# A spectral filter beside a gated feed-forward layer: half-length inverse products over the columns, a separate path for column 256, and 64x64 tiles for the 32-point steps

## Chip, cores and metric

One core of one Trainium2 chip. The metric is device microseconds (us) of one execution; each kernel is run several times, and each run has a state, fast or slow. Engines: PE is TensorE, DVE is VectorE, ACT is ScalarE, POOL is GpSimd, SP is SyncE, which here only issues DMAs.

## The reference

```python
def reference(A_x, A_w_r, A_w_i, B_x, B_w_gate, B_w_up, B_w_down):
    # x: (1, 2048, 512) bf16; w_r, w_i: (2048, 257); gate, up: 512 x 1792; down: 1792 x 512
    xn = layernorm(A_x)
    X = rfft2(xn)                                   # over tokens (2048) and columns (512)
    a = irfft2(X * (w_r + 1j * w_i), s=(2048, 512))
    g, u = xn @ B_w_gate, xn @ B_w_up
    return A_x + a + (gelu(g) * u) @ B_w_down       # tanh gelu
    # [types, casts and the set-up of the inputs are cut]
```

## The kernel before

The feed-forward part is a regular stream on PE: for each of four blocks of 512 tokens and each of 14 slices of the inner width a gate group, then an up group (four matmuls of 512 columns each), with the down groups in between. The Fourier part is cut into units, placed at numbered gaps of this stream, called **hooks** (0 to 156). In a trace, hook n is where the stream's n-th group ends.

- D: forward transform over the 512 columns (real input: 257 frequencies, kd).
- A: 64-point step over the tokens. Its result goes to a scratch in HBM and is read back transposed (`tv`).
- B: 32-point step, ends the forward transform. Then the filter on DVE. C: 32-point step, starts the inverse; second trip through HBM (`vv`).
- E: 64-point step; F: inverse transform over kd; DVE adds the result.

```python
def load_late(dst, src, keys):                      # later loads: GpSimd's queue, not before the PE work ahead of it
    op("pool", lambda e: e.dma_start(dst, src), w=keys, dma=True, after=[("pe", pr.cnt["pe"])])

def unit_A(j):
    ...                                             # [matmuls cut]
    op("act", ... activation(t4[:], pair(bk), ACT.Copy, scale=SC_A), ...)
    dma("sp", scr1.rearrange(...)[j], t4[:], r=[("tt", j % 4)], w=[("scr1", j)])
    if j >= 3:
        load_tv(j - 3)                              # [the last three after j = 15]

def unit_B(h):                                      # 128x64 tiles, two at once
    for ri in range(2):
        for hh in range(2):
            e.matmul(bank(bk + ri)[64 * hh:64 * hh + 64, 0:257], be[:, 64 * ri:64 * ri + 64], tv[:, 16 * hh + h, :], ...)
    # waits for all of tv; then ACT evicts, and DVE makes two products and two sums with Wr, Wi

def unit_C(h):                                      # 64x128 tiles, two at once
    for ri in range(2):
        for hh in range(2):
            e.matmul(bank(bk + hh)[:, 0:257], cm[64 * hh:64 * hh + 64, h, ri, :], y[64 * hh:64 * hh + 64, ri, 0:KD], ...)

def unit_F(j):                                      # four products of 256 columns
    e.matmul(bank(bk)[:, 0:256], z[:, 0, :], gm[:, 0, :], ...)
    e.matmul(bank(bk)[:, 0:256], z[:, 1, :], gm[:, 1, :], ...)
    e.matmul(bank(bk)[:, 256:512], z[:, 2, :], gm[:, 2, :], ...)
    e.matmul(bank(bk)[:, 256:512], z[:, 3, :], gm[:, 3, :], ...)

# places: filter loads (16 of them, on GpSimd) from hook 26; the first B at 54, C from 61, E from 113, F from 117
xv = A_x.rearrange("o (q b j) d -> b q (o j) d", b=2, j=NJ)   # order of tokens: runs of j are contiguous in HBM
```

## Time and profile before

| | before |
|---|---|
| time, median of the runs taken with the changed kernel's | 196.56 us (196.11 to 200.26, 4 runs, the longest of them slow) |
| span of the profiled run, granted clock | 194.3 us, 1.0 |
| PE busy | 186.9 us, 96% |
| last hook (156) ends at | 188.2 us |
| filter loads | 16, issued by GpSimd |

Read it in this order: busy share per engine (who could be the bound), the 40 slices (where it isn't), the waits (who stops whom), then the timeline of the bound engine for the real price of its instructions. The prediction shows those lines.

### The profile page before, as it was taken

How to read it: one execution, taken by the hardware profiler on the slowest of the kernel's cores; microseconds unless marked ns; L12 is line 12 of the kernel's file. 1: busy time of each engine (PE TensorE's matmuls, PEld its weight loads, DVE VectorE, ACT ScalarE, POOL GpSimd, SP SyncE). 2: the span in 40 equal slices, each digit the busy share in tenths (PEclk: the TensorE clock that was granted, in tenths of full speed). 3: DMA queues.
4: the chain of work that ended last, by engine and by line, in shares of the span. 5: the costliest groups of instructions: out<-in, count | busy, mean ns of one | idle time of the engine just before them, and what ended most of it. 6: DMA issues, size and time to landing. Idle time of an engine off the chain costs nothing.

```text
span 194.3 us, 3181 instructions
## 1 busy us (share of the span) xinstructions
PE 186.9 (96%) x1173; PEld 95.4 (49%) x1173; DVE 112.1 (58%) x266; ACT 89.1 (46%) x160; POOL 26.3 (14%) x52
## 2 busy tenths in 40 slices
PE   7599898999999999999999999999999999999993
PEld 2285454646454444444444444444455555555562
DVE  2759899787722227658577556423146656546361
ACT  3144465666466124547446363413454555644310
POOL 0200515023200232222300000000011011111000
DMA  4999999556655663355862331340002221121112
GB/s 125 326 290 333 285 255 255 144 145 129 139 162 142 145 119 90 75 95 129 177 168 86 108 112 35 104 120 17 1 0 54 54 59 27 42 53 45 26 28 54
DMA packets 19167, 23.09 MB, mean 119 GB/s; under 512 B 2240, under 2 KB 16832, under 8 KB 18768
## 3 DMA queue, kind: packets, MB, share of 16 engines
q1 hardware_dynamic: 16064, 16.46, 31.4%
q0 software_dynamic: 1712, 5.32, 12.5%
q10 hardware_dynamic: 1376, 1.11, 2.0%
q8 instruction: 9, 0.15, 0.3%
q14 instruction: 6, 0.05, 0.1%
HBM read 16.57 MB, written 6.31 MB: 118 GB/s over the span
## 4 chain that ended last, share of the span: by engine, by line
PE 85%; DVE 7%; DMA 4%; issue 1%; SPq 1%; POOL 1%; ACT 0%; DVEq 0%
PE ps L642 24%; PE ps L600 22%; PE ps L585 22%; DMA wu<-in_B_w_up_dram 4%; DVE st L351 3%; PE ps L462 2%; PE ps L488 2%; PE ps L522 2%; PE ps L622 2%; DVE hT L606 1%; PE ps L373 1%; SPq L304 1%; PE ps L437 1%; PE ps L548 1%; PE ps L550 1%
## 5 line engine op out<-in xcount | busy, mean ns | idle before, releaser
L606 DVE TENSOR_TENSOR hT<-ps,gl 128x512 bf16<-128x512 f32 (+1 forms) x59 | 39.0, 662 | 38.5 <-PE ps L600 36.9
L585 PE MATMUL ps<-xnT,wg 128*128 128x512 f16 (+1 forms) x236 | 58.1, 369 | 0.8 <-ACT xnT L385 0.8
L600 PE MATMUL ps<-xnT,wu 128*128 128x512 f16 (+1 forms) x236 | 58.1, 368 | 0.2 <-DMA wu<-in_B_w_up_dram 0.2
L588 ACT ACTIVATE gl<-ps 128x512 bf16<-128x512 f32 (+1 forms) x59 | 34.0, 575 | 45.0 <-PE ps L585 44.0
L642 PE MATMUL ps<-wd,hT 128*128 128x512 bf16 x210 | 50.1, 379 | 0.0
L600 PEld LDWEIGHTS ps<-xnT,wu 128*128 128x128 bf16 x236 | 22.4, 98 | 21.9 <-issue 0.8
L585 PEld LDWEIGHTS ps<-xnT,wg 128*128 128x128 bf16 x236 | 21.8, 98 | 21.8 <-issue 2.8
L642 PEld LDWEIGHTS ps<-wd,hT 128*128 128x128 bf16 x210 | 19.8, 98 | 21.1 <-issue 0.8
L657 DVE TENSOR_TENSOR x_sb<-ps,x_sb 128x512 bf16<-128x512 f32 x12 | 8.3, 690 | 16.4 <-PE ps L642 16.4
L530 POOL COPY zt<-xn 1x128 bf16<-1x128 bf16 x16 | 4.9, 309 | 80.4 <-DMA xn<-row 42.5
L556 ACT ACTIVATE eo<-ps 128x512 bf16<-128x512 f32 x16 | 9.5, 595 | 12.4 <-PE ps L551 12.4
L529 ACT ACTIVATE zt<-ps 128x512 bf16<-128x512 f32 x16 | 9.5, 596 | 7.7 <-PE ps L522 7.6
L468 ACT ACTIVATE xc<-ps 128x514 f16<-128x514 f32 x16 | 8.7, 600 | 8.8 <-PE ps L462 8.8
L351 DVE BATCH_NORM_STATS2 st<-x_sb 128x6 f32<-128x512 bf16 x16 | 10.8, 684 | 3.0 <-DMA x_sb<-in_A_x_dram 3.0
L494 ACT ACTIVATE vp<-ps 128x514 bf16<-128x514 f32 x16 | 8.7, 598 | 6.2 <-PE ps L488 6.2
L561 DVE TENSOR_TENSOR ys<-eo 128x256 bf16<-128x256 bf16 x16 | 4.6, 289 | 11.9 <-ACT eo L556 11.9
L447 ACT ACTIVATE tt<-ps 128x514 f16<-128x514 f32 x16 | 8.7, 597 | 6.0 <-PE ps L441 6.0
L420 ACT ACTIVATE xs<-ps 128x512 f16<-128x512 f32 x16 | 9.6, 597 | 4.1 <-PE ps L416 4.1
L359 POOL TENSOR_TENSOR rstd<-vpe,mhalf 128x4 f32<-128x4 f32 (+1 forms) x5 | 4.6, 921 | 31.0 <-DVE vpe L358 31.0
L308 POOL DMA_DIRECT2D Wr<-in_A_w_r_dram x8 | 5.0, 625 | 19.2 <-PE ps L642 13.4
L363 DVE TENSOR_SCALAR xn<-x_sb,ag,rstd 128x512 f16<-128x512 bf16 x16 | 6.2, 435 | 2.0 <-POOL rstd L359 2.0
L308 POOL DMA_DIRECT2D Wi<-in_A_w_i_dram x8 | 4.9, 617 | 13.0 <-PE ps L585 10.1
(68 smaller groups left out, 169.6 us busy)
## 6 DMA issues: line engine op xcount, KB each, us to landing
scr<-tt SPq DMA_DIRECT2D x16, 128.5 KB
tv<-scr SPq DMA_DIRECT2D x16, 128.5 KB
scr<-vp SPq DMA_DIRECT2D x16, 128.5 KB
arena<-scr SPq DMA_DIRECT2D x16, 128.5 KB
out_dram<-osb SPq DMA_DIRECT2D x30, 64.0 KB
x_sb<-in_A_x_dram SPq DMA_DIRECT2D x6, 256.0 KB, 14.1
Wr<-in_A_w_r_dram POOLq DMA_DIRECT2D x8, 128.5 KB, 4.7
Wi<-in_A_w_i_dram POOLq DMA_DIRECT2D x8, 128.5 KB, 4.3
```

The costliest lines, as they stand in the source:

```text
L308: op("pool", lambda e: e.dma_start(dst, src), w=keys, dma=True, after=[("pe", pr.cnt["pe"])])
L351: op("dve", lambda e: e.bn_stats(st[:, j, :], x_sb[:, j, :]), r=[("x", j, 0), ("x", j, 1)], w=[("st", j)])
L420: op("act", lambda e: e.activation(x4[:].rearrange("p (a c r) -> p a c r", a=2, r=4), bank(bk).rearrange("p (a r c) -> p a c r", a=2, r=4) ...
L447: op("act", lambda e: e.activation(t4[:], pair(bk), ACT.Copy, scale=SC_A), r=[("ps", bk), ("ps", bk + 1)], w=[("tt", j % 4)])
L468: op("act", lambda e: e.activation(xc[s2][:, :, 0:KD], pair(bk), ACT.Copy, scale=SC_B), r=[("ps", bk), ("ps", bk + 1)], w=[("xc", s2)])
L529: op("act", lambda e: e.activation(z[:], bank(bk).rearrange("p (a c) -> p a c", a=4), ACT.Copy, scale=SC_E), r=[("ps", bk)], w=[zk])
L556: op("act", lambda e: e.activation(o2[:], bank(bk), ACT.Copy), r=[("ps", bk)], w=[ok])
L585: ins = e.matmul(bank(bg)[:, 0:n], wg_sb[:, dc, fc * P:(fc + 1) * P], xnT[:, dc, c0:c0 + n], start=(dc == 0), stop=(dc == 3))
L588: op("act", lambda e: e.activation(gl[k % 3][:, 0:n], bank(bg)[:, 0:n], ACT.Gelu_apprx_tanh), r=[("ps", bg)], w=[("gl", k % 3)])
L600: ins = e.matmul(bank(bu)[:, 0:n], wu_sb[:, dc, fc * P:(fc + 1) * P], xnT[:, dc, c0:c0 + n], start=(dc == 0), stop=(dc == 3))
L606: op("dve", lambda e: e.tensor_tensor(hT[b % 2][:, fc, h0:h0 + n], bank(bu)[:, 0:n], gl[k % 3][:, 0:n], ALU.mult), r=[("ps", bu), ("gl", k ...
L642: ins = e.matmul(bank(bk), hT[b % 2][:, fc, jj * P:(jj + 1) * P], wd_sb[:, fc, :], start=(fc == 0), stop=(fc == NFC - 1))
```

## The change

The intent is to give PE less to stream. F folds a second time: with all angles taken half a sample off, the 256 outputs of each parity follow from 128 columns and their mirror, so its products have 128 columns. Column 256 would spoil the even sizes, so it is taken out of the main path and walks a narrow one of its own ("mini", four small steps). With 256 columns left, B and C fit 64x64 tiles, four at a time; B of a slice and C of the slice before share a hook, so PE changes its tiling less often. The filter is loaded in eight slices, once for the rows of the real parts and once for those of the imaginary parts; the loads now go out on SP's queue. The four loads of C's constants (256 KB each, on GpSimd) move too, from hooks 34, 52, 62 and 72 to hooks 46 to 52. To make the halves of a tile neighbours, the order of tokens changes.

```diff
-    xv = A_x.rearrange("o (q b j) d -> b q (o j) d", b=2, j=NJ)
+    xv = A_x.rearrange("o (q j b) d -> b q (o j) d", b=2, j=NJ)
 [constants, buffers and the narrow path cut]
+        def load_tv(m):                                   # once per four units of A
+            for r in range(2):
+                dma("sp", tv[64 * r + 16 * m:64 * r + 16 * m + 16]..., scr1[8 * m:8 * m + 8, 64 * r:64 * r + 64]..., ...)
+        def load_W(s):                                    # 8 loads a slice, 64 in all
+            for k, src in enumerate((A_w_r, A_w_i)):
+                for c in range(2):
+                    for i in range(2):                    # the same rows of HBM twice
+                        p0 = 64 * c + 32 * i
+                        yield (load_late, W[k][s % 4][p0:p0 + 32, :, :, 0:KW], v[c][:, :, hs, :], ..., "sp")
 unit_B
+                        ins = e.matmul(bank(bk + r)[64 * c:64 * c + 64, 256 * hh:256 * hh + 256], be[64 * r:64 * r + 64, 0:64],
+                                       tv[64 * r:64 * r + 64, 16 * c + 2 * g + hh, :], ...)
 unit_F
+                for a in range(4):
+                    ins = e.matmul(bank(bk)[:, a * P:(a + 1) * P], z[:, a, :], gm[:, a, :], ...)
 places
+        for s, h0 in enumerate((26, 31, 36, 41, 55, 60, 66, 71)):     # filter slices
+        for g in range(9):
+            h = int(52 + 5.5 * g)                         # B of slice g and C of slice g - 1
-            at(113 + 2.5 * j, (unit_E, j))
+            at(107 + 2.5 * j, (unit_E, j))
```

## The prediction

> **What bounds the kernel now.** I read the page first: busy time per engine, the 40 slices, the chain that ended last.
>
> ```profile
> PE 186.9 (96%) x1173; PEld 95.4 (49%) x1173; DVE 112.1 (58%) x266; ACT 89.1 (46%) x160; POOL 26.3 (14%) x52
> ...
> PE   7599898999999999999999999999999999999993
> ...
> DVE  2759899787722227658577556423146656546361
> ...
> PE 85%; DVE 7%; DMA 4%; issue 1%; SPq 1%; POOL 1%; ACT 0%; DVEq 0%
> ```
>
> TensorE (PE) is busy in every slice after the first 30 us or so; VectorE (DVE) is near full only in slices 3 to 8 (10 to 40 us), where layer norm and fold run. The waits agree: what idle time there is belongs to ACT and DVE, waiting for PE; the rows in which PE waits sum to about 4 us (1.7+1.2+0.8+0.5+0.2), and in stretches of ten us PE is busy 10.00 from 40 us to 190. So time is saved here only by giving PE less to stream, and only after about 40 us surely.
>
> PE's busy time overlaps itself (matmuls are pipelined), so a matmul's own duration is not its price. The price is the distance from one start to the next, and that is read from the timeline of PE. A stretch with the inverse transform (L522 is the E step, L548 to L551 the F step over kd):
>
> ```profile
> 151.46 0.39 PE L522 MATMUL ps<-be,arena 128*128 128x128 f16 x4
> 151.69 1.03 PE L585 MATMUL ps<-xnT,wg 128*128 128x512 f16 x4
> 152.55 1.03 PE L600 MATMUL ps<-xnT,wu 128*128 128x512 f16 x4
> 153.41 0.27 PE L548 MATMUL ps<-gm,zt 128*128 128x256 f16 x1
> 153.52 0.27 PE L549 MATMUL ps<-gm,zt 128*128 128x256 f16 x1
> 153.63 0.27 PE L550 MATMUL ps<-gm,zt 128*128 128x256 f16 x1
> 153.74 0.27 PE L551 MATMUL ps<-gm,zt 128*128 128x256 f16 x1
> 153.85 1.03 PE L585 MATMUL ps<-xnT,wg 128*128 128x512 f16 x4
> ```
>
> Columns: start, length, engine, line. 512 columns cost (152.55-151.69)/4 = 0.216 us, 256 columns 0.11 us, 128 columns (151.69-151.46)/4 = 0.057 us. A stretch with the 32-point steps (L462 is B in 128x64 tiles, L488 is C in 64x128 tiles):
>
> ```profile
> 83.80 0.81 PE L585 MATMUL ps<-xnT,wg 128*128 128x512 f16 x3
> 84.53 0.63 PE L462 MATMUL ps<-tv,be 128*64 128x257 f16 x8
> 85.10 1.04 PE L600 MATMUL ps<-xnT,wu 128*128 128x512 f16 x4
> ...
> 86.84 1.03 PE L600 MATMUL ps<-xnT,wu 128*128 128x512 f16 x4
> 87.80 0.62 PE L488 MATMUL ps<-yy,cm 64*128 64x257 bf16 x8
> 88.35 1.04 PE L585 MATMUL ps<-xnT,wg 128*128 128x512 f16 x4
> ```
>
> Eight matmuls of 257 columns take 0.57 us, not 8 x 0.11: two tiles run at once, so there are four waves of 0.11. And each visit to a tile shape has a toll: B should start at 83.80+3x0.216 = 84.45 and starts at 84.53 (0.08), and stays 0.57-0.44 = 0.13 longer than its waves: 0.21 us. For C 0.10+0.11, the same 0.21.
>
> **What the Trainium skill says.** "TensorEngine Tiling (Array Packing)", section Tiling Modes: a 64x64 split gives four independent tiles, and changing the tiling mode (not just the tile) drains the engine. The trace agrees on the drain: 0.21 us per visit. It shows two tiles at once, never four. "TensorE: Matmul & The Clock Gate", section Part 3, says tiles of different row and column groups overlap and reports 3.07x for four row tiles; no run here shows it for 64x64. The same tiling page, section Tile-to-Partition Mapping, says column tiling turns off the fast weight load; in the trace before, the 128x64 weight loads last 109 ns against 98 ns for 128x128 and delay nothing. "VectorE: DVE Perf Modes", section Mode 2x_1P, asks for 16-bit data, step +1 or -1 and 4-byte alignment for two results a cycle; the adds here (256 columns 0.29 us, 512 0.425, 1024 0.685) run at 0.52 ns an element, which fits two a cycle. The new mirrored write has step -1 and may or may not keep it.
>
> **The change part by part, on PE.**
> 1. F: 64 matmuls go from 256 to 128 columns. Same count, all late, all in a saturated stretch: 64 x (0.11-0.057) = **-3.4 us**.
> 2. B: 64 matmuls remain, but four at once instead of two: 32 waves become 16. 16 x 0.11 = **-1.8 us**, if four tiles really run at once.
> 3. C: 64 matmuls in pairs become 128 of half the width in fours: 32 waves before and after, 0.
> 4. Visits. Before: A in 8 pairs, B 8, C 8, the row of column 256 once: 25. After: A in 4 groups; B of a slice and C of the slice before it stand in one hook and share the 64x64 shape: 9 visits, the second of the four narrow steps among them; the three other narrow steps: 3. 16. 9 x 0.21 = **-1.9 us**. A's four (0.8 us) fall before 63 us, partly where PE waits for DVE anyway; I count half: -1.5.
> 5. The narrow path of column 256: 4+4+16+1 matmuls of 16 to 64 columns, in 2+1+4+1 waves, one row matmul removed: seven waves. I take the 128-column price, 0.057 us, as the price of one: **+0.4 us**.
> Sum: -3.4-1.8-1.5+0.4 = -6.3 us. D, E, the gate, up and down matmuls (47+48+46 us of stream by the starts) are unchanged.
>
> **Beside PE.** DVE: the filter was 16 x (2x0.425+2x0.29) = 22.9 us and becomes 16 products of 1024 elements, 16 x 0.69 = 11 us, the combining sum having moved into C's products. The finish gets two more half-width operations per tile, 32 x 0.29 = 9.3 us (11.5 if the mirrored one runs at one element a cycle), plus about 2 us of narrow work. Even, within 2 us. It moves work from 80-115 us to 135-180 us, where DVE was at 5.2 to 5.7 us in ten; about four tiles in ten us add 2.3 to 2.8: at most 8.5 in ten. Not the bound. ACT: 48 evictions of 0.60 us become 24 of 1024 elements; from 0.597 for 512 and 0.383 for 256 the slope is 0.84 ns an element, so 1.02 us each: 24.5 us instead of 28.7. Fewer, but each holds two PSUM banks longer, and B and C now queue two of them at one hook.
>
> **Rivals.**
> (a) *Four tiles don't run at once*, or their weight loads (twice as many per column streamed) don't keep up. If both steps went at the present pair rate, B saves nothing and C's 64 waves cost 3.5 us more: gain about 1 us, time near 195. For it: nothing here shows four at once. Against it: A, B and C all reach full pair overlap with loads issued 2 to 4 ns apart. One in seven.
> (b) *A DMA round trip becomes the wait.* B needs all of the transposed tile, E all of the second one, and both now come sooner after their last producer. E: C's last unit moves from about 123 to about 121.5 us on the old clock, and E's first from 137 to 132. From C's end: eviction to 123.5, write issued 124 and landed about 3 us later (the old last read went out at 129.6 after a write issued at 125.6), read issued and landed about 3.2 us after: 130.3. Slack 1.7 us. B: last A at 62.5, second eviction 64.1, write landed 67, two reads behind the filter's loads, landed 70.8; B's hook is at 71.6. Slack 0.8 us. The 64 filter loads now go out by SP's queue, at 0.36 to 0.6 us of issue each (30 us in all) in the same stretch, in order, ahead of those reads. A stall of 1 to 3 us is possible: one in five.
> (c) *PSUM banks.* With B and C in one hook ACT owes 2 us; the next gate's gelu is 2 us late. Four banks remain, which last PE two gates and two ups, 3.4 us. No stall, or a few tenths.
> (d) *The early stretch moves.* x is now read in rows of 1 KB instead of 2 to 4 KB; packets of 1024 bytes took about 50 ns and 4096 about 200, so bytes count and not packets. I expect +-0.3 us.
>
> **Range.** The sum says -6.3; I put -0.4 us of it back for small stalls of (b), (c) and (d): 196.4-5.9 = 190.5 us, 3% faster. The good end is all tolls saved and nothing lost: 188.9. The bad end is one stall of (b) or half of (a): 193.6. The 2% line is at 192.5: two of its three ways to be missed, (a) and a long (b), have about one in five together.
>
> **What would show it.** F's lines at 0.057 us from start to start; B and C together about 0.21+0.21+0.45 = 0.87 us a visit, starts in fours a few ns apart; about 16 visits; PE idle at no hook. PE's stream from first to last start some 6 us shorter, the tail after the last matmul unchanged (3 us). Wrong would be: starts within B or C 0.05 us apart instead of in fours (a); a wait of B for the read of the first scratch, or of E for the second (b); gate or up waiting for ACT or DVE after a B/C visit (c); a first gate later than before (d).

## More of the kernel before

One more view matters later, the issue timeline of SP where the first scratch makes its last trip (start, length, engine, line, what, count):

```profile
61.94 0.44 SPq L304 DMA_DIRECT2D scr<-tt  x1
62.42 4.06 SPq L304 DMA_DIRECT2D tv<-scr  x4
```

The last write goes out at 61.94 us; nothing of the filter stands in this queue.

## The result, and the profile after

The changed kernel is correct and takes **203.52 us** (median of 4 runs, 203.14 to 204.27) against 196.56 us: slower, ratio 1.0323, 95% interval 1.0246 to 1.04. A ratio here is the mean time of one kernel's fast runs over that of the other's of the same rounds, so it is not quite the ratio of the medians quoted. All runs of the changed kernel were fast; the profiled one has a span of 202.5 us and a granted clock of 0.965 instead of 1.0.

The page after (busy time, the slices of PE and of its clock, the chain that ended last):

```profile
PE 185.2 (91%) x1261; PEld 94.7 (47%) x1261; DVE 112.2 (55%) x261; ACT 86.2 (43%) x136; POOL 23.6 (12%) x69
...
PE   7689996999999970599999999999999999999994
...
PEclk9969999999999997569999999999999999999999
...
PE 76%; DMA 9%; SPq 9%; DVE 3%; issue 1%; DVEq 0%
```

PE is still the engine with most work, and has *less* of it. But slices 15 to 17 (counted from 0) show a hole, the clock falls there and once near the start, and SP's queue is now 9% of the chain. The hole in the waits (us in total, times, longest), in the chain (start, length, what) and in stretches (PE, PEld, DVE, ACT, POOL busy, then clock, DMA share, GB/s):

```profile
PE ps L568 <- DMA tv<-scr: 8.7, 1, 8.7
```

```profile
71.70 0.88 PE ps L687 x4
75.61 7.36 DMA tv<-scr
83.85 3.95 PE ps L743 x9
```

```profile
74.50:83.00 8.50, 0.01 (x1) 0.00 (x0) 0.00 (x0) 0.00 (x0) 1.28 (x3) 0.76 0.65 168
83.00:89.20 6.20, 5.99 (x21) 2.17 (x22) 1.99 (x3) 1.02 (x1) 0.00 (x0) 0.51 0.09 37
```

The first B waits 8.7 us for the read of the first scratch, once. Then PE runs at half clock: the trace grants it 0.5 from 78.89 us for 10.24 us, and 512 columns take 0.427 us instead of 0.216 until 89.1. From 83.2 to 89.1 that loses another 3.0 us. Why the read is late is on SP's issue timeline:

```profile
65.81 2.54 SPq L340 DMA_DIRECT2D W<-in_A_w_i_dram  x4
68.39 1.25 SPq L340 DMA_DIRECT2D W<-in_A_w_r_dram  x2
69.68 1.14 SPq L337 DMA_DIRECT2D scr<-early  x2
70.87 1.29 SPq L340 DMA_DIRECT2D W<-in_A_w_r_dram  x2
72.20 2.56 SPq L340 DMA_DIRECT2D W<-in_A_w_i_dram  x4
74.86 1.44 SPq L337 DMA_DIRECT2D tv<-scr  x2
```

SP issues without a gap, 0.64 us per filter load. The last evictions of A end at 64.6 and 65.6 us, but their writes go out at 69.7 and 70.3; they land at 72.5 and 73.2; the two reads go out at 74.9 and 75.6 and land at 81.5 and 83.0.

The predicted savings are there all the same. Two stretches of PE's timeline after (L646 is F; L568 is B, L593 is C):

```profile
157.63 1.03 PE L687 MATMUL ps<-xnT,wg 128*128 128x512 f16 x4
158.50 0.39 PE L646 MATMUL ps<-gm,tv 128*128 128x128 f16 x4
158.72 1.03 PE L702 MATMUL ps<-xnT,wu 128*128 128x512 f16 x4
```

```profile
90.09 1.03 PE L687 MATMUL ps<-xnT,wg 128*128 128x512 f16 x4
91.05 0.41 PE L568 MATMUL ps<-tv,be 64*64 64x256 f16 x8
91.29 0.61 PE L593 MATMUL ps<-early,cmx 64*64 64x256 bf16 x16
91.83 1.04 PE L702 MATMUL ps<-xnT,wu 128*128 128x512 f16 x4
```

F costs (158.72-158.50)/4 = 0.055 us a matmul. B and C together take from 90.09+4x0.216 = 90.95 to 91.83, 0.88 us; their matmuls start in fours, 3 ns apart.

How far each hook of the changed kernel lags behind the same hook of the one before gives the account:

| stretch | lag grows by | what it is |
|---|---|---|
| up to hook 0 | +2.8 us | later start |
| hooks 0 to 52 | +0.1 | D and A: nothing saved |
| hooks 52 to 156 | +5.2 | wait +8.7, half clock +3.0; the rest, -6.5, is work saved |
| hook 156 | 8.1 in all | the spans differ by 202.5-194.3 = 8.2 |

So the saving came; 14.5 us were added beside it, in two places.

### The profile page after: what moved, and what is told of

Read it like the earlier page. It is cut to its first block, busy times and chain, and to the rows that moved or that the text cites.

```text
span 202.5 us, 3402 instructions
## 1 busy us (share of the span) xinstructions
PE 185.2 (91%) x1261; PEld 94.7 (47%) x1261; DVE 112.2 (55%) x261; ACT 86.2 (43%) x136; POOL 23.6 (12%) x69
## 4 chain that ended last, share of the span: by engine, by line
PE 76%; DMA 9%; SPq 9%; DVE 3%; issue 1%; DVEq 0%
PE ps L743 23%; PE ps L687 20%; PE ps L702 20%; SPq L337 8%; DMA x_sb<-in_A_x_dram 6%; DMA tv<-scr 4%; PE ps L593 2%; PE ps L646 2%; PE ps L617 2%; PE ps L723 2%; PE ps L568 1%; SPq L340 1%; DVE st L382 1%; PE ps L404 1%; PE ps L472 1%
## 5 line engine op out<-in xcount | busy, mean ns | idle before, releaser
L687 PE MATMUL ps<-xnT,wg 128*128 128x512 f16 (+1 forms) x236 | 59.3, 375 | 1.0 <-DMA wg<-in_B_w_gate_dram 1.0
L579 DVE TENSOR_TENSOR early<-early,W 128x1024 bf16<-128x1024 f16 x16 | 10.3, 686 | 14.0 <-ACT early L574 14.0
L574 ACT ACTIVATE early<-ps 128x1024 f16<-128x1024 f32 x8 | 8.2, 1021 | 19.7 <-PE ps L568 19.7
L758 DVE TENSOR_TENSOR x_sb<-ps,x_sb 128x512 bf16<-128x512 f32 x11 | 7.6, 691 | 14.3 <-PE ps L743 14.1
L449 ACT ACTIVATE early<-ps 128x512 f16<-128x512 f32 x16 | 9.5, 596 | 9.8 <-PE ps L445 9.8
L652 ACT ACTIVATE tv<-ps 128x512 bf16<-128x512 f32 x16 | 9.5, 596 | 8.2 <-PE ps L646 8.2
L626 POOL COPY tv<-tv 1x128 bf16<-1x128 bf16 x16 | 5.0, 314 | 60.3 <-ACT tv L624 60.3
L624 ACT ACTIVATE tv<-ps 128x512 bf16<-128x512 f32 x16 | 9.5, 595 | 5.0 <-PE ps L617 5.0
L568 PE MATMUL ps<-tv,be 64*64 64x256 f16 x64 | 3.5, 296 | 8.7 <-DMA tv<-scr 8.7
L557 POOL COPY w<-W 128x4 bf16<-128x4 bf16 x16 | 3.9, 245 | 47.3 <-DMA W<-in_A_w_i_dram 25.2
L598 ACT ACTIVATE early<-ps 128x1024 bf16<-128x1024 f32 x8 | 8.2, 1024 | 0.8 <-PE ps L593 0.8
L480 ACT ACTIVATE early<-ps 128x1024 f16<-128x1024 f32 x8 | 7.8, 1021 | 0.0
L377 PE MATMUL ps<-dumm 128*128 128x512 f16 x14 | 6.2, 632 | 1.2 <-DVE dumm L349 1.2
## 6 DMA issues: line engine op xcount, KB each, us to landing
arena<-c_am SPq DMA_DIRECT2D x1, 1024.0 KB, 12.8
```

The costliest lines, as they stand in the source:

```text
L449: op("act", lambda e: e.activation(x4.rearrange("p (a c r) -> p a c r", a=2, r=4), bank(bk).rearrange("p (a r c) -> p a c r", a=2, r=4), A ...
L574: op("act", lambda e: e.activation(xc[i].rearrange("p r hh c -> p (r hh c)"), pair(bk), ACT.Copy, scale=SC_B), r=[("ps", bk), ("ps", bk + ...
L579: op("dve", lambda e, k=k: e.tensor_tensor(pp[i][k], xc[i], W[k][g % 4][:, :, :, 0:256], ALU.mult), r=[("xc", i)] + [key for c in range(2) ...
L624: op("act", lambda e: e.activation(z, bank(bk).rearrange("p (a c) -> p a c", a=4), ACT.Copy, scale=SC_E), r=[("ps", bk)], w=[zk] + (TVK if ...
L652: op("act", lambda e: e.activation(o2, bank(bk), ACT.Copy), r=[("ps", bk)], w=[ok] + (TVK if j < 2 else []))
L687: ins = e.matmul(bank(bg)[:, 0:n], wg_sb[:, dc, fc * P:(fc + 1) * P], xnT[:, dc, c0:c0 + n], start=(dc == 0), stop=(dc == 3))
```

## The experiments

Seventeen kernels were run; each fast-run ratio is against the kernel before on the same chip. Three gave wrong outputs.

**Theory:** the first scratch's round trip (A, eviction, write, read, B) became the path that sets the end because the filter loads stand ahead of it in SP's queue, which issues in order. **Rival 1:** the loads' traffic slows write and read in the DMA engines, whichever queue they come from. **Rival 2:** the trip is simply that long, alone or not. Beside these, the start: the new token order, or chance.

### SP freed in two ways, with the traffic left, and another layout

**e1_w_behind** moves filter slices 2 and 3 behind the last A.

```diff
-        for s, h0 in enumerate((26, 31, 36, 41, 55, 60, 66, 71)):
+        for s, h0 in enumerate((26, 31, 45, 49, 55, 60, 66, 71)):
```

> The changed kernel with one edit: the filter loads of slices 2 and 3 are issued after the last read of the first scratch instead of ahead of it. Theory 1 (SP issues in order, and 16 filter loads of 0.64 us each stand ahead of the last scratch writes and reads): the two last writes are issued at about 64.7 and 66 us instead of 69.7 and 70.3, the two last reads at about 69 instead of 74.9, they land near 76, PE waits under 2.5 us for them instead of 8.7, its clock stays full after that, and the time is about 193.8 us. Theory 2 (the filter's traffic or the slow 16 KB reads are the cause, whatever the order): PE still waits 6 us or more and the time is 200 or more.

Measured 200.29 us, ratio 1.0143 (1.0073 to 1.0213). Its waits:

```profile
PE ps L568 <- DMA tv<-scr: 5.1, 1, 5.1
```

The writes now go out as soon as the evictions end (64.64 and 65.56 us) and land at 68.8. But the reads, issued at 68.9 and 69.6, land at 74.8 and 79.3, with the DMA engines 95% busy from 69.6 us on. The 16 filter loads now go out just behind the reads, from 70.3 to 80.7 us, so they are out of the way in the queue and not in the DMA engines; and all four loads of C's constants (1 MB, on GpSimd) go out from 69.1 to 74.8 us beside them. The order is part of it: 8.7 becomes 5.1.

**e2_w_pool** leaves the places and moves all filter loads to GpSimd's queue.

```diff
-   yield (load_late, W[k][s % 4][...], v[c][:, :, hs, :], [...], [...], "sp")
+   yield (load_late, W[k][s % 4][...], v[c][:, :, hs, :], [...], [...], "pool")
```

> The changed kernel with all 64 filter loads issued from GpSimd's queue at the same places of the schedule: same bytes, same shape, about the same moments, but SP's queue is free. Theory 1: as with the loads moved, 193 to 196 us, PE's wait for the first scratch under 2.5 us. Theory 2 (traffic): wait and time as in the changed kernel, 203.5 us.

Measured 203.82 us, ratio 1.0367.

```profile
PE ps L568 <- DMA tv<-scr: 9.4, 1, 9.4
```

SP is free, the writes go out at 64.6 and 65.5 us, and yet land only at 71.1 and 73.1; the reads land at 80.2 and 83.6. The theory of SP's order alone falls. The Trainium skill has this in "DMA: Bandwidth & Descriptors", section Issuing engines are not separate DMA queues: transfers from SP, ACT and GpSimd end on the same 16 engines and interleave. Here it cost the whole of what the free queue had gained.

**e6_read16** gives the scratch a layout in which the reads are contiguous on 16 partitions.

```diff
-    scr1 = nc.dram_tensor("scr1", (32, P, KD), F16).ap()
+    scr1 = nc.dram_tensor("scr1", (2, 32, 64, KD), F16).ap()
-                    scr1[8 * m:8 * m + 8, 64 * r:64 * r + 64].rearrange("l (i x) c -> l i (x c)", i=2),
+                    scr1[r, 8 * m:8 * m + 8].rearrange("l (i x) c -> (l i) (x c)", i=2),
 [and the write of 128 partitions becomes two of 64]
```

> The changed kernel with the first scratch laid out so that each of its reads is one contiguous 256 KB block, as the reads of the second scratch are (16 landings of the semaphore instead of 8 and one early); the writes are split in two. The order of SP's queue is as in the changed kernel. If the slow read (5 to 7.4 us from issue to landing against 3.7 to 4.3 us of the second scratch's) is a part of the wait of its own, the reads land in about 4 us, PE's wait falls from 8.7 to about 6 us and the time to about 200. If the order in SP's queue is all, 203.5.

A miss: 205.92 us, ratio 1.0418, and the reads still took 7.0 and 7.7 us, the wait 9.8. The idea came from the trace's semaphore updates: a read of the changed kernel gives nine, eight of them with data, a read of this layout gives 16. It is not what was slow.

### The start, and the half clock

**e3_tokens** puts the old token order back (constants permuted to match).

```diff
-    xv = A_x.rearrange("o (q j b) d -> b q (o j) d", b=2, j=NJ)
+    xv = A_x.rearrange("o (q b j) d -> b q (o j) d", b=2, j=NJ)
 [out, three constants, E's columns and one copy likewise]
```

> The changed kernel with the old order of tokens (x is read and stored as in the kernel before, 2 to 4 KB in a row at load; constants permuted to match, result still right). Theory: the 1 KB rows of x delay the first weights and idle PE into the half clock, 2.8 us at the start; without them the first full gate ends near 15.2 us less some tenths instead of 15.8 at hook 0 (13.05 in the kernel before), and the time is 2 to 3 us less, about 200.9. Rival (the start differs by chance or by the order of SP's queue): 203.5, no change.

Measured 200.75 us, ratio 1.0193. Hook 0 ends at 12.8 us instead of 15.8, as in the kernel before (13.0), and no half clock is left at the start; the wait at B stays (9.8).

**e4_warm** puts 36 dummy matmuls of 512 columns ahead of the first B.

```diff
+                    for _ in range(36):
+                        ins = e.matmul(bank(bw), dumm[:, 0:128], dumm[:], start=True, stop=True)
```

> The changed kernel with 36 dummy matmuls (7.8 us) ahead of the first B step, where PE sits idle 8.7 us. Theory: the second part of the loss is the half clock that follows the idle time (5.9 us at half speed, 2.9 us lost); with PE kept busy the clock stays at 1.0, B starts no later, and the time is about 200.7. Rival (the clock dip has another cause or costs nothing): 203.5.

Measured 202.8 us over all runs, but two of five were slow; the fast ones (200.2, 200.39, 202.8) give a ratio of 1.0167 against 1.0323. The clock stays 1.0 through the hole. (The profile is of a slow run.) The difference is 1.6%, some 3 us, as worked out above, but the two ratios come from different chips and their intervals (1.01 to 1.0235, 1.0246 to 1.04) only just part. The Trainium skill, "TensorE: Matmul & The Clock Gate", section Part 1, says that an idle window of about 3.4 us halves the clock. The half-clock stretches of these traces last 3.41, 6.83 or 10.24 us, one to three such windows, which agrees. But a hole in PE's work need not be so long: one of 2.6 us (e8) and one of 2.7 (e11) were followed by half clock, one of 2.2 (e14) and one of 2.9 (e9) were not. No sharp limit comes out of these runs.

### Later B, and both causes at once

**e5_late_b** and **e7_late_tok** (this with the old token order too) start B nine hooks later.

```diff
-            h = int(52 + 5.5 * g)
+            h = int(61 + 4.4 * g)
```

> The changed kernel with one number edited: the B and C steps start at hook 61 and come every 4.4 hooks instead of at 52 and every 5.5; they end at the same hook. All loads keep their order and traffic, PE only has other work until the transposed tile has landed (83 us; hook 61 is reached at about 84). Theory 1 (8.7 us of wait and 2.9 us of half clock behind it are lost at this one place, and all else of the prediction holds): no wait of PE for the first scratch, clock 1.0 after 16 us, time 203.5-8.7-2.9 = 191.9 us. Rival (the time lost there is lost again further on, at E's read of the second scratch or at the filter): 196 or more.

> B and C from hook 61 and the old order of tokens together: both losses taken away, nothing else. If they are all that went wrong, 203.5-11.6-2.75 = 189.2 us, inside the range predicted, 7 us under the kernel before. If anything else was lost, above 191.5.

Both outputs were wrong: filter slice 4 reuses the buffer of slice 0 and is now loaded ahead of the first product. 201.64 us (ratio 1.0222) and 200.24 us (1.014). The wait at B was still 1.9 and 4.2 us, and a new one came at C, up to 3.1 and 4.2 us; for these the trace names no releaser, but DVE, whose products C needs, waited 12 to 13 us in all for filter loads, the overwritten slice among them. They say only that room alone is not enough while the filter flows: the reads took 8.0 to 9.7 us. (e7's profile fell in a slow run.)

**e8_quiet** takes both causes away at the first B: old token order, the layout of e6, filter slices 2 to 7 at hooks (51, 55, 60, 64, 69, 73), C's constants at (36, 53, 58, 63).

> B left at hook 52: old order of tokens, reads of the first scratch contiguous, the filter loads of slices 2 to 7 issued only after the last of these reads, three of four loads of C's constants later too. Last read issued near 66 us and landed near 70 against B's hook at 70.6: no wait or under 1 us, clock 1.0, 189 to 190 us. If SP's queue can't keep up with 48 filter loads of 0.64 us in the shorter stretch, DVE waits for filter slices and PE for DVE at the C steps: 191 or more.

Correct, 198.59 us, ratio 1.0054 (0.9966 to 1.0142).

```profile
PE ps L618 <- DMA arena<-scr: 2.6, 1, 2.6
...
PE ps L569 <- DMA tv<-scr: 1.2, 1, 1.2
```

The wait at B is 1.2 us and the clock stays whole there. But 48 filter loads now stand in SP's queue while C writes the second scratch, whose trips then end late: E waits 2.6 us, and the clock halves for 3.41 us. (e17 below differs from e8 only in the queue of these 48 loads and in their hooks, by one; its wait at B is the same, and E waits 1.0 us instead of 2.6.) This run also had a late start (hook 0 at 17.9 us) in the old token order.

### Measuring the terms of the sum

**e9_pairs** loads the filter in slices of four rows, half as many loads, the first half early, at hooks 24 and 28, in the old token order; C's constants move to hooks 36, 55, 60 and 66 and B to 54. **e10_f256**, **e11_apart** and **e12_newtok** are e9 with one thing changed: F streams 256 columns per product (wrong); C stands one hook behind B; the new token order.

```diff
 e9_pairs
-        for s, h0 in enumerate((26, 31, 36, 41, 55, 60, 66, 71)):
+        for s, h0 in enumerate((24, 28, 60, 71)):
-            h = int(52 + 5.5 * g)
+            h = int(54 + 5.25 * g)
 e10_f256
-   ins = e.matmul(bank(bk)[:, a * P:(a + 1) * P], z[:, a, :], gm[:, a, :], ...)
+   ins = e.matmul(bank(bk)[:, a // 2 * 256:a // 2 * 256 + 256], z[:, a, :], gm[:, a // 2 * 2:a // 2 * 2 + 2, :]..., ...)
 e11_apart
-                at(h, (unit_C, g - 1))
+                at(h + 1, (unit_C, g - 1))
```

> The changed kernel repaired, result right: old order of tokens; filter loads of four rows instead of two, so 32 instead of 64 issues in SP's queue, the first 16 of them done before the last A step, the other 16 after B has begun; C's constants loaded around the last reads of the first scratch; B from hook 54 every 5.25 hooks, ends where it did. If the two places found (start, first B) are all that kept the change from its gain: no wait of PE above 1 us after 10 us, clock 1.0 throughout, 203.5-2.75-11.6 = 189.2 us, 3.5 to 4% under the kernel before. If a third loss is hidden behind them, 192 or more.

> The repaired kernel with F's 64 matmuls streaming 256 columns again, as in the kernel before (result wrong on purpose: each product also runs over its neighbour's constants). It measures what the halving of F is worth: 64 x (0.109-0.056) = 3.4 us more than the repaired kernel, about 192.6. If F's matmuls hide beside something, less than 1 us.

> The repaired kernel with C one hook after B instead of in the same hook: same matmuls, same shapes, but B and C visit the 64x64 shape apart, 16 visits instead of 9. If a visit costs 0.21 us of drain, 7 x 0.21 = 1.5 us more, about 190.7. If the drain is hidden, no change.

> The repaired kernel with the new order of tokens (x in rows of 1 KB at load), so the one difference to the repaired kernel is the order of tokens, on the same chip in the same call. If the rows of 1 KB cost the start, 2 to 3 us more, about 192, and a clock of 0.5 for 3.4 or 6.8 us near 10 us. If the late start is chance of the DMA engines (one kernel with the old order had it too), no difference.

e9 is a miss: 206.47 us, ratio 1.036. The early filter loads kept the DMA engines 95% busy from 40 to 60 us, the two reads of the *second* quarter of the scratch, issued at 48.4 and 49.1 us, landed only at 57.9 and 61.9, and one write kept SP 6.5 us in issue; the wait at B was 8.7, at E 2.9 (8.6 and 2.9 in e12, whose profile is of a fast run; those of e9 and e11 fell in slow ones). Traffic moved forward only meets an earlier trip.

The two probes still measure, in stretches at full clock. From hook 120 to 156 twelve F units run: 38.58 us in the changed kernel, e9, e13, e15, e16 and e17 alike, 41.14 in e10. 2.56/48 matmuls = 0.053 us each for the 128 columns: **64 x 0.053 = 3.4 us**. From hook 58 to 90 e9 takes 34.23 us (e13 the same), e11 35.62: 1.39 us for six more visits of the tile shape, 0.23 each: **0.21 holds, within 0.02**. e10 and e11 as a whole took 213.18 and 207.99 us, with more waits and half clock than e9, so whole times say less. e12 took 209.08 us, ratio 1.0541 (1.0459 to 1.0622) against 1.036 (1.0286 to 1.0434): on the same chip the new token order is slower by some 3.6 us here too. Where it loses them is not shown, since the profile of e9 starts late as well (hook 0 at 15.6 us, in e12 at 16.3).

### The version with nothing in the way

**e13_mix** is e8 with filter slices 2 to 7 issued by GpSimd, from hook 52 on, and B three hooks later. The lines below are against the changed kernel.

```diff
 [token order of e3, layout of e6]
-   yield (load_late, W[k][s % 4][...], ..., "sp")
+   yield (load_late, W[k][s % 4][...], ..., "sp" if s < 2 else "pool")
-        for s, h0 in enumerate((26, 31, 36, 41, 55, 60, 66, 71)):
+        for s, h0 in enumerate((26, 31, 52, 56, 60, 64, 68, 72)):
-        for i, h0 in enumerate((46, 48, 50, 52)):
+        for i, h0 in enumerate((36, 53, 58, 63)):
-            h = int(52 + 5.5 * g)
+            h = int(55 + 5.1 * g)
```

> The changed kernel with the old token order, contiguous scratch reads, filter slices 0 and 1 early on SP, slices 2 to 7 issued by GpSimd from the first B on (so nothing of the filter stands ahead of or beside the first scratch round trip, and nothing of it stands ahead of the later ones on SP). Theory (SP order and traffic together): no wait over 1.5 us at the first B, none over 1 us at E, clock 1.0 there; 189 to 191 us where the start is good, 192 where it is late with a half clock near 10 us; ratio to before 0.96 to 0.98. Rival (the round trip is long by itself, whatever else runs): wait at B stays above 4 us and the ratio above 1.0.

**190.98 us** (6 runs, 189.51 to 191.19), ratio **0.9708** (0.9681 to 0.9735): faster than both kernels. Its page (slices of PE and of the clock), SP's issues and PE at the first B:

```profile
PE   7599997999999999999999999997999999999993
...
PEclk9999999999999999999999999999999999999999
```

```profile
61.53 2.63 SPq L337 DMA_DIRECT2D scr<-early  x4
66.29 0.77 SPq L337 DMA_DIRECT2D tv<-scr  x2
```

```profile
73.16 1.03 PE L688 MATMUL ps<-xnT,wg 128*128 128x512 f16 x4
74.11 0.41 PE L569 MATMUL ps<-tv,be 64*64 64x256 f16 x8
74.46 1.04 PE L703 MATMUL ps<-xnT,wu 128*128 128x512 f16 x4
```

B follows its gate with no hole. The only waits left that PE has for a scratch are 1.4 us at E. From hook 0 to hook 156 it takes 170.2 us, the kernel before 175.2; with the 1.4 us of E added back the work saved is 6.4 us, where the prediction's sum said 6.3.

**e14_mixnew** is e13 with the change's token order, **e15_start** e13 with nine dummy matmuls spread over the start.

> e13_mix with the change's token order (x in 1 KB rows). If this order costs the start: hook 0 ends 2 to 3 us later than in e13_mix and the time is 2 to 3 us longer. If the late start is chance: same as e13_mix within 1 us.

> e13_mix plus nine dummy matmuls spread ahead of the first transposes, gate and up. If the half clock near 10 us follows from PE's idleness there, it goes, and the time falls by 1 to 2 us where e13_mix shows it; if e13_mix starts without it, no change (within 0.5 us).

e14: 195.05 us, ratio 0.9911, some 4 us more than e13 in the same job. Hook 0 ends at 15.5 us instead of 12.9, and E's wait is 2.2 instead of 1.4. The stretch from 8 to 12 us in e13, then in e14 (columns as above):

```profile
8.00:12.00 4.00, 3.18 (x34) 2.54 (x32) 2.48 (x10) 1.76 (x4) 0.70 (x1) 1.00 1.09 278
```

```profile
8.00:12.00 4.00, 2.40 (x17) 1.45 (x18) 1.84 (x7) 0.98 (x2) 0.70 (x1) 0.74 1.12 274
```

Half the matmuls, at a lower clock, with as many bytes moving. In all eight traces with 1 KB rows of x, the second piece of the gate weights lands whole at 13.2 to 13.9 us; in seven of the eleven with the old order at 8.9 to 9.9, but in the other four (e8, e9, e11, e16) at 11.2 to 14.3. So the new order brings late weights every time, and the old one has them sometimes. Hook 0 follows only roughly: it ends at 14.0 to 16.9 us with 1 KB rows, and in the old order at 12.8 to 13.4 in seven traces but at 14.5 to 17.9 in e8, e9, e10 and e17, two of which had their weights early. Which DMA engine straggles, and why, stays open.

e15: 190.29 us, ratio 0.9693, the same as e13, whose start had no half clock to take away. Whether dummies cure a late start is not shown.

**e16_layout** is e13 with the change's own scratch layout; **e17_slot** is e13 with the first B back at its hook 52.

> e13_mix with the change's own layout of the first scratch. In the alone-tested e6_read16 the layout was worth nothing. If that holds: same as e13_mix within 1 us (190 to 192), and the read of the first scratch takes the same 4 to 6 us. If the 64-partition form of the read is slow by itself: a wait of 1 to 3 us at the first B and 1 to 3 us more time.

> e13_mix with the first B at the change's own place, three units (some 3.4 us) earlier. In e13_mix the last part of the read landed at 72.65 us while that place comes at 71.4 us. Theory (even undisturbed the round trip is longer than the predicted slack): a wait of about 1.2 us at the first B, no half clock or a short one, 191 to 193 us. Rival (undisturbed it fits as predicted): no wait, 190.5 us or less.

e16: 192.01 us, ratio 0.9738 (0.9663 to 0.9813), not told apart from e13; no wait at B. The reads took 4.9 and 6.4 us, against 4.5 and 6.0 in e13. The layout does not matter, as e6 said.

e17: 193.26 us, ratio 0.979 (0.9711 to 0.9869). Its PE timeline at the first B, with the idle time before it in brackets:

```profile
73.47 0.41 PE L569 MATMUL ps<-tv,be 64*64 64x256 f16 x8 [1.25 <-DMA tv<-scr]
```

Even with the queue to itself and hardly a transfer beside it the trip ends 1.25 us after B's place. (Whole times of e17 and e13 are not told apart; the wait is read from the trace.) So rival 2 has a small share too: the change put B about one microsecond too early for the trip at its best.

What the parts are worth: from 1.0323 (the change) to 0.9911 (e14) everything around the round trip, about 8 us; from there to 0.9708 (e13) the token order, about 4 us. Within the first part, order and traffic cannot be split into two shares that add: with SP freed and the traffic left (e1, e2) 5.1 and 9.4 us of waiting remained, with both taken away 1.2 (e8) or none (e13, which also gives the trip three hooks more). No run takes the traffic away and leaves the order. And "traffic" is not the filter alone: in the changed kernel two of the four loads of C's constants go out at 72.1 and 72.7 us, between the last writes and the last reads of the scratch, and land at 76.6 and 78.4; in e2 all four go out beside the reads, as in e1. e8 and e13 move three of the four behind the trip and one ahead of it, together with the filter. How much of the traffic's share is theirs is not shown.

## Why the prediction was wrong, point by point

- **F, -3.4 us.** Right: 0.055 us a matmul, and e10 measured 3.4 us.
- **B, -1.8 us, four tiles at once.** Right: starts 3 ns apart in fours; a visit of B and C takes 0.88 us where 0.87 was said. Rival (a) is out.
- **Visits at 0.21 us.** Right by e11. The half of A's four that I counted did not show: hooks 0 to 52, where the first narrow step (hook 46) now lies too, took 0.1 us *more* than before.
- **Narrow path, +0.4 us.** Not measured as a whole; its step of 16 matmuls took 0.33 us in e13, visit and all, where the prices used make 0.44.
- **Sum -6.3 us.** Work saved on PE: 6.5 us in the changed kernel, 6.4 in e13. The good end of the range, 188.9, does not come out of the sum: with all of A's visits it gives -6.7, or 189.7.
- **DVE, ACT, PSUM (rival c).** Right: DVE at most 8.2 us in ten where F runs, and the larger eviction 1.02 us as estimated; no wait of PE on them after a visit.
- **Rival (b), "write landed 67, two reads behind the filter's loads, landed 70.8 ... Slack 0.8 us".** This is the step that failed. Said: 6.7 us from the second eviction to the reads. Measured: 65.56 to 82.97, 17.4 us. The terms: 4.8 us before the write is issued, because SP is behind by that much (said: none); 2.9 for the write (as said); 2.4 until the second read is issued; 7.4 from issue to landing (said: about 3.2). I had the queue's load, 0.36 to 0.6 us an issue, in the same paragraph (measured 0.64, some 41 us for the 64 and not 30), and never laid the issues end to end on a time line. And the 3.2 us leaned on the second scratch, whose last read in the trace of before went from 129.6 to 133.2 us; the reads of the *first* one in that trace took 5.4, 5.6 and 6.6 us for the last three, at half the size. Undisturbed, e13's took 4.5 and 6.0.
- **"A stall of 1 to 3 us is possible".** Mis-sized by its consequence as well: the clock halved 4.4 us into the 8.7 us hole, and the half clock cost 3.0 us more after it. I had no term for it.
- **Rival (d), "bytes count and not packets. I expect +-0.3 us".** Wrong: hook 0 came 2.8 us later, and e3, and e14 against e13, tie most of it to the token order.
- **E's slack of 1.7 us.** Its lines were misread: from 125.6 to 129.6 us are 4.0 for the write and not "about 3", and the read took 3.6 (to 133.2) and not 3.2, which leaves a slack of about 0.4. In the changed kernel E did not wait; with SP laden later (e8) it did, 2.6 us, and even e13 shows 1.4. The slack was thinner than said.

So the mechanism named for the gain was right in every term that was measured by itself; the price of two side conditions, when a transfer is issued and how long it takes among others, was not worked out with the same care. The one in five given to (b) had the right event at a quarter of its size.

## What to carry to other kernels

When work moves closer to its producer across a trip through HBM, write the trip out as a chain with four terms (issue queue, write, issue queue, read), lay every DMA of that queue end to end beside it, and take landing times from transfers of the same kind under the same load. Neither another queue (e2, 9.4 us of waiting left) nor a better order (e1, 5.1) was enough alone where the loads both stood in the way and shared the engines; a load that can wait should be issued after the trip, by an engine that has no trip to make. And count a hole of some us on PE (here 2.6 us could be enough) at its length plus half of the half-clock time that is left when it ends: 8.7 + 5.9/2 us here.

## What the Trainium skill lacked or had wrong

- "TensorEngine Tiling (Array Packing)", Key Properties, says that a change of tiling mode drains TensorE, but no cost: here 0.21 us per visit of another shape by the timeline, 0.23 by e11.
- No page found has a measurement of 64x64 tiles that run at once; here 64x64 matmuls started 3 to 4 ns apart in fours, and four of 256 columns took 0.11 to 0.12 us together.
- "DMA: Bandwidth & Descriptors", Anatomy of one DMA, gives a transfer issued from GpSimd as about 2 us plus bytes over the full rate, which is 2.6 us for 256 KB (an estimate from that page), and no such sum for SP; here loads of 256 KB from GpSimd (C's constants in the changed kernel) landed 3.5 to 5.7 us after issue, and reads of 256 KB from SP 4.5 and 6.0 us after issue with little beside them (e13) and 5.9 to 9.8 us beside the filter loads (the changed kernel, e1, e2, e6).
- No page found gives the issue time of a DMA on SP for many short rows: 0.64 us for a load of 64 KB in rows of 514 bytes, so 64 of them hold the queue for about 41 us.
- "TensorE: Matmul & The Clock Gate", Part 1, has the clock at half speed after at least one idle window of about 3.4 us. Here a hole of 2.6 us (e8) was enough once, and one of 2.9 (e9) was not; after one of 8.7 us the half clock lasted 10.24 us.
